# Two key chunks of x loaded one by one, and six steps' attention numerators formed by features in column tiles

## The chip, the cores and the metric

The kernel runs on one core of a Trainium2 chip. The metric is the time of one execution in device microseconds; the time before is the median of three runs. The core has a matrix engine (TensorE; PE in the profile, its weight loads PEld), a vector engine (VectorE, DVE), an engine for activations (ScalarE, ACT), GpSimd (POOL) and a queue engine that issues transfers (SyncE, SP). TensorE multiplies a stationary operand (the weights, loaded first) by a moving one, column by column, and writes to PSUM, a memory of eight banks of 512 float32 per partition.

## The reference

Two attention blocks read the same x (2048 tokens, 640 features, 32 heads of 20 features), and a gate mixes their outputs.

```python
g = sigmoid((x * gate_w).sum(-1))                 # one gate per token
# block A: linear attention, features softmax(p) and softmax(-p), p = (q or k) @ w_phi
kv, z = sum_s phi_k[s] v[s], sum_s phi_k[s]
a = (phi_q @ kv / (phi_q @ z + 1e-6)) @ wo_A
# block B: four segments of 512 tokens
logits = q @ k.T * 20**-0.5 + causal_mask         # within the segment
a_dot = softmax(logits) @ v
a_mem = (phi(q) @ M) / (phi(q) @ z + 1e-6)        # phi(t) = t + 1 if t > 0 else exp(t)
o = sig(beta) * a_mem + (1 - sig(beta)) * a_dot   # then M, z += phi(k).T v, sum phi(k)
b = o @ wo_B
out = g * a + (1 - g) * b
```

## The kernel before, in words

Every engine executes its instructions in the order in which the program emits them (`manual_schedule`), so the order of the work is written out by hand. The parts, in order of time:

**The start (to about 11 us).** The key weights come in five chunks of 128 rows (`wnat_k`, three on ScalarE's queue, two on SP's), and the first 512 tokens of x are wanted as keys early. A string of two-letter steps (line 319) lists the work of the start: `T` transposes a weight chunk on TensorE (line 181) and copies it out, `M` multiplies a transposed chunk with the masked `w_phi` (line 189; "the fold"), `X0` transposes two key chunks of x (line 200), `k` and `v` are the key and value products of a chunk (line 242). The letter `a` or `d` behind a number says whether ScalarE or VectorE copies the result out. x for `X0` comes in one load on SP's queue (line 107), behind `w_phi` and two weight chunks and ahead of the gate vector, the value weights (line 111) and the transposing loads of x (line 114). All PSUM tiles of this part come from one pool, `aps`, of four pairs of banks, and a tile takes a pair that came free.

**Block A (to about 127 us).** For 16 chunks, keys and values, their exponentials (line 253) and normalised features (line 261); then the sums `kv` (line 393, where TensorE is split into two column tiles of 64 columns), query features (line 420), and numerators and denominators (lines 478, 496). For the last of these the pool `aps` is closed and four others take its banks, `nps0`, `nps1` and `nps2` for numerators and `pps` for projections of block B; they lie in the order in which a tuple lists them.

**Block B (127 to 303 us).** There are 32 steps: four segments by eight groups of four heads. Two steps make a double step, 16 of them. A double step emits five bursts of scores: each burst is two PSUM tiles filled by products with 32 rows (line 757, four row tiles) and read by one exponential each on ScalarE (line 761, 128x1024); GpSimd then clears the triangle above the diagonal (line 768). The probabilities of a step are kept by key chunk, keys on the partitions: chunk c against the queries from 128c on.

Between the bursts stand items from a string per double step (`PLAN`, line 971): `A` to `D` are the numerators and memory products of a step, `h` halves of the next segment's projections (line 943), `f` and `o` halves of the output projections (line 887), `t` a transposing transfer of finished output rows, `x`, `y`, `k`, `q` and `z` parts of the feature maps. `A` and `D` belong to the first step of the double step, `B` and `C` to the second step of the double step before. Each item has a weight in microseconds, and `SHARES` says what share of the weights may be emitted before each next burst.

The numerators of a step (`pv_items`, line 811) are, for four query chunks j and four heads i, products over the key chunks c up to j: 40 in all, with 128 probabilities as weights and 21 columns moving (20 value features and a column of ones, whose sum is the denominator). Results have queries on the partitions, in one bank of the tile `nda`. The other bank takes the memory products (`mem_items`, lines 819 and 824). Then `emit_epi` divides: a reciprocal (line 836), a product with the gates (838), the scaling of both parts (848, on VectorE) and their sum into `oB` (851, mostly GpSimd); for three segments it also updates the memory (854 to 858).

**The end (303 us on).** `u` in the plan issues four transposing transfers (line 981) of the last segment's first 384 output columns, which the last products (line 1067) read; the last step and the last rows follow.

Of the kernel before, what the change touches and what calls it, by code (L numbers as in the profile page):

```python
# [15 lines left out]
def kernel(  # L16
# [82 lines left out]
    nc.sync.dma_start(out=Wc, in_=A_w_phi.rearrange("h f g -> (h f) g").rearrange("(c p) g -> p c g", p=P))  # L99

    for what in "w1 w3 x0 g v0 v1".split():
        n = int(what[1:]) if len(what) > 1 else 0
        if what[0] == "w":
            nc.sync.dma_start(out=wnat_k[:, n], in_=wsrc(D)[:, n])
        elif what[0] == "x":
            x_nat[n] = xload.tile([P, 2, D], BF16, name="x_nat")
            nc.sync.dma_start(out=x_nat[n], in_=x2[0:512].rearrange("(m r) d -> m r d", r=4)[:, 2 * n:2 * n + 2])
# [44 lines left out]
    for j, eng in ((0, nc.vector), (1, nc.gpsimd), (2, nc.vector), (3, nc.gpsimd), (4, nc.gpsimd)):  # L152
        emit_Wphi(j, eng)
# [21 lines left out]
    def w2tile(name):  # L175
        return aps.tile([P, 2, 512], F32, name=name, tag="w2")
# [18 lines left out]
    def emit_xT(n):  # L195
        pair = w2tile("xtp")
        tps = [pair[:, u].bitcast(BF16)[:, 0:D].rearrange("p (c t) -> p c t", c=KC) for u in range(2)]
        for u in range(2):
            for c in range(KC):
                nc.tensor.transpose(out=tps[u][:, c, :], in_=x_nat[n][:, u, c * P:(c + 1) * P], identity=ident_b)  # L200
        for u in range(2):
            nc.vector.tensor_copy(out=xP[:, :, (2 * n + u) * P:(2 * n + u + 1) * P], in_=tps[u])
# [116 lines left out]
    for step in "T0a T2d M0a T1d M2a T4d M1a T3d X0 M4a M3a k0 g k1 v0 v1 r0 r1".split():  # L319
        n = int(step[1:2] or 0)  # L320
        if step[0] == "T":
            emit_foldT(wnat_k, WkT, n, {"a": nc.scalar.copy, "d": nc.vector.tensor_copy}[step[2]])
        elif step[0] == "M":
            emit_foldM(WkT, WkA, n, {"a": nc.scalar.copy, "d": nc.vector.tensor_copy}[step[2]])
        elif step[0] == "X":
            emit_xT(n)
        elif step[0] == "k":
# [130 lines left out]
    vBs = [resB.tile([P, 4, H, DH + 1], BF16, name=f"vB{n}") for n in range(2)]  # L458
# [110 lines left out]
    def emit_zsum():  # L569
        emit_zz(emit_z(z_den[:, 0]))  # L570
        open_stages()
        for vB in vBs:
            nc.gpsimd.memset(vB[:, :, :, DH:DH + 1], 1.0)

# [5 lines left out]
    for what in "ppppvzppppdvp":  # L580
# [16 lines left out]
        for n in ('nps1', 'pps', 'nps0', 'nps2')}  # L597
# [109 lines left out]
    with ExitStack() as bctx:  # L707
# [7 lines left out]
            for n in ('bnd', 'st_b', 'bps', 'st_a')}  # L715
# [18 lines left out]

        class Step:
            def __init__(self, k):
                self.s, self.g = divmod(k, G)
                self.PT = {}
                self.last = k == NSEG * G - 1
                self.nda = nda  # L740
# [73 lines left out]

        def mem_items(st):
# [15 lines left out]
        def emit_epi(st):  # L831
# [14 lines left out]
            else:  # L846
# [4 lines left out]
                eng.tensor_tensor(out=oview, in0=tdv[:, 0], in1=tdv[:, 1], op=ALU.add)  # L851
            if s < NSEG - 1:
# [84 lines left out]

        def half_item(part, sc, half):
# [17 lines left out]
        def half_items(s, order):  # L956
# [14 lines left out]
        PLAN = ("qhhhyzhokxooAD", "qhhByhChkzoxAooD", "qhhByhChkzxoAooD",  # L971
                "ooBqoyokCozxoADo", "hkhBhhChhqhyAhDztt", "khhBxhhqChfhyzAD",
                "khhBxhhqCfyzADt", "khhBxhhqChfyhzAD", "khhxtBhhqChyhADzt",
                "hhBhhqChfyhzAD", "hhBhhqCfhyzAthD", "hhBhhqhCftyhzAD",
                "fBftCfftAD", "ffBtCfftAD", "fBtfCffADf", "fBCuffAffD")
        SHARES = [[0.2, 0.42, 0.55, 0.78], [0.19, 0.4, 0.6, 0.84], [0.2, 0.4, 0.6, 0.81], [0.19, 0.38, 0.59, 0.78], [0.19, 0.38, 0.58, 0.81], [0.18, 0.41, 0.65, 0.86], [0.2, 0.4, 0.6, 0.83], [0.19, 0.4, 0.6, 0.83], [0.2, 0.4, 0.6, 0.8], [0.22, 0.39, 0.6, 0.82], [0.19, 0.39, 0.61, 0.82], [0.2, 0.39, 0.6, 0.82], [0.2, 0.4, 0.6, 0.8], [0.21, 0.4, 0.61, 0.8], [0.19, 0.37, 0.59, 0.82], [0.2, 0.41, 0.6, 0.84]]
# [10 lines left out]
        for dstep in range(NSEG * G // 2):  # L987
# [5 lines left out]
            for w in PLAN[dstep]:  # L993
# [177 lines left out]
```

## Time and profile before

| | |
|---|---|
| median of 3 runs | 316.44 us (316.29 to 316.65) |
| profiled execution | 315.58 us |
| its span in the profile | 313.6 us |
| TensorE, ScalarE busy | 303.6 us, 252.0 us |
| VectorE, GpSimd busy | 224.0 us, 206.8 us |
| granted TensorE clock | 1.0 |

A row of a group shows the line, engine and operation, the tile written and those read, shapes, then the count, busy time and the mean duration in ns of one; behind the second bar stands the idle time of the engine just before, and what ended it. A row of the timeline starts with the start and the length in us from the span's start; a number after `x` says how many instructions were merged. Matmuls overlap and their ends are modelled, so the price of a run of them is read from its first start to the start of what follows.

### The profile page before, as it was taken

What the parts mean: (1) busy time and instruction counts of PE and PEld (TensorE: products, weight loads), DVE (VectorE), ACT (ScalarE), POOL (GpSimd) and SP (SyncE); (2) the same over time, 40 slices, a digit from 0 to 9 for tenths busy, and PEclk for the clock granted to TensorE, in tenths of its full rate; (3) what the DMA queues carried; (4) which work ended last, traced back from release to release, by engine and by line L of the source; (5) the groups of instructions that cost most, each with busy time, mean ns of one, the idle gap of its engine ahead of it and who ended that gap; (6) DMA issues with size and microseconds to landing.
All of it is one profiled execution on the core that took longest, in us unless ns stands there. A gap on an engine that the chain in (4) does not pass through costs nothing.

```text
span 313.6 us, 10096 instructions
## 1 busy us (share of the span) xinstructions
PE 303.6 (97%) x4182; PEld 208.4 (66%) x4182; DVE 224.0 (71%) x508; ACT 252.0 (80%) x320; POOL 206.8 (66%) x308
## 2 busy tenths in 40 slices
PE   8999999999999999999999999999999999999995
PEld 7788877755578778465666666565666666565673
DVE  3477997999779997677758588777755765455553
ACT  4677888267846648999998999999998898998953
POOL 8588599103247989955657577688786877666550
PEclk9999999999999999999999999999999999999999
DMA  7989944439217998775421394473745545222132
GB/s 216 199 184 204 210 108 129 127 89 365 74 36 106 130 136 147 135 100 99 55 50 36 69 127 86 59 120 69 110 84 78 86 100 72 64 78 53 48 90 84
DMA packets 94007, 34.56 MB, mean 110 GB/s; under 512 B 82442, under 2 KB 93834, under 8 KB 93962
## 3 DMA queue, kind: packets, MB, share of 16 engines
q1 hardware_dynamic: 93386, 33.28, 54.4%
q10 hardware_dynamic: 576, 0.66, 0.7%
q8 instruction: 32, 0.52, 0.7%
q14 instruction: 13, 0.11, 0.1%
HBM read 6.10 MB, written 2.62 MB: 28 GB/s over the span
## 4 chain that ended last, share of the span: by engine, by line
PE 69%; ACT 19%; DVE 4%; POOL 3%; issue 2%; DMA 1%; ACTq 0%; DVEq 0%; POOLq 0%
ACT PT L761 16%; PE proj L943 10%; PE st_ps L757 10%; PE proj L887 9%; PE pk L242 7%; PE pq L420 7%; PE nda L811 7%; PE pv L242 7%; PE proj L557 3%; PE num L478 2%; PE kv_ps L393 2%; DVE tt L527 1%; DMA oTA<-oA 1%; POOL oA L686 1%; DVE rr L503 1%
## 5 line engine op out<-in xcount | busy, mean ns | idle before, releaser
L761 ACT ACTIVATE PT<-st_ps 128x1024 bf16<-128x1024 f32 x160 | 153.9, 1023 | 12.2 <-PE st_ps L757 9.8
L768 POOL TENSOR_SCALAR_AFFINE_SELECT PT<-PT 128x512 bf16<-128x512 bf16 (+1 forms) x130 | 84.4, 668 | 46.7 <-ACT PT L761 46.3
L811 PEld LDWEIGHTS <-PT 128*128 128x128 bf16 x1280 | 40.0, 96 | 9.0 <-issue 5.4
L811 PE MATMUL nda<-vB,PT 128*128 128x21 bf16 x1240 | 41.5, 173 | 0.1
L261 POOL TENSOR_TENSOR EkSn<-Ek,krec 128x1280 bf16<-128x1280 bf16 x15 | 35.1, 2360 | 9.2 <-DVE krec L260 7.3
L943 PEld LDWEIGHTS <-xTf 128*128 128x128 bf16 x300 | 26.5, 97 | 13.8 <-issue 5.3
L949 DVE CAST Z<-proj 128x320 bf16<-128x320 f32 x44 | 21.1, 488 | 16.7 <-PE proj L943 15.6
L427 ACT ACTIVATE Eq<-pq 128x1024 bf16<-128x1024 f32 x20 | 19.4, 1021 | 12.2 <-PE pq L420 12.2
L257 DVE TENSOR_REDUCE ksum<-Ek 128x64 f32<-128x1280 bf16 x16 | 23.6, 1474 | 7.2 <-ACT Ek L253 7.2
L527 DVE TENSOR_TENSOR tt<-num,rr 128x640 f32<-128x640 f32 x32 | 25.0, 812 | 4.6 <-POOL rr L520 1.8
L686 POOL TENSOR_TENSOR oA<-tt 128x640 bf16<-128x640 f32 x16 | 24.6, 1545 | 5.3 <-DVE tt L527 5.0
L887 PE MATMUL proj<-WkA,oTA 128*128 128x320 bf16 x160 | 28.0, 300 | 0.0
L757 PE MATMUL st_ps<-Z 32*128 32x512 bf16 (+3 forms) x256 | 24.9, 299 | 3.0 <-ACT PT L761 2.5
L253 ACT ACTIVATE Ek<-pk 128x640 bf16<-128x640 f32 x32 | 20.8, 703 | 7.9 <-PE pk L242 6.8
L757 PE MATMUL st_ps<-Eq 32*128 32x512 bf16 (+3 forms) x256 | 25.2, 299 | 1.5 <-ACT PT L761 1.2
L242 PEld LDWEIGHTS <-xTf 128*128 128x128 bf16 x200 | 22.6, 113 | 4.7
L851 POOL TENSOR_TENSOR oB<-td 128x320 bf16<-128x320 f32 x22 | 19.6, 889 | 4.4 <-DVE td L848 3.6
L420 PE MATMUL pq<-xTf,WqA 128*128 128x512 bf16 x100 | 22.4, 379 | 0.0
L887 PE MATMUL proj<-WvA,oT 128*128 128x320 bf16 x120 | 21.3, 300 | 0.0
L848 DVE TENSOR_TENSOR td<-nda,rec 128x640 f32<-128x640 f32 x23 | 19.0, 825 | 2.5 <-DVE rec L838 0.5
L836 DVE RECIPROCAL rec<-nda 128x32 f32<-128x32 f32 (+1 forms) x31 | 10.3, 331 | 12.8 <-PE nda L824 8.1
L887 PEld LDWEIGHTS <-oTA 128*128 128x128 bf16 x160 | 13.6, 97 | 8.3 <-issue 4.2
(183 smaller groups left out, 558.8 us busy)
## 6 DMA issues: line engine op xcount, KB each, us to landing
Z<-EkSn SPq DMA_DIRECT2D x32, 160.0 KB, 2.8
out_dram<-orow SPq DMA_DIRECT2D x8, 160.0 KB, 1.9
out_dram<-oTA SPq DMA_DIRECT2D x6, 160.0 KB, 1.8
WvA<-in_A_wqkv_dram SPq DMA_DIRECT2D x2, 400.0 KB, 6.4
WvB<-in_B_wv_dram SPq DMA_DIRECT2D x1, 800.0 KB, 4.7
WkB<-in_B_wk_dram SPq DMA_DIRECT2D x1, 800.0 KB, 6.5
WqB<-in_B_wq_dram SPq DMA_DIRECT2D x1, 800.0 KB, 8.2
WkA<-in_A_wo_dram SPq DMA_DIRECT2D x1, 800.0 KB, 11.3
```

What stands on the lines that cost most here:

```text
L242: nc.tensor.matmul(ps[:, bk, 0:n], lhsT=key_tokens(c, sc), rhs=rhs, start=(c == 0), stop=(c == by_row[-1][0] if sc == 0 and W is WkA else ...
L257: nc.vector.tensor_reduce(out=ksum, in_=Ek.rearrange("p s (h f) -> p (s h) f", f=DH), axis=AX.X, op=ALU.add)
L261: (nc.vector if sc == NCH - 1 else nc.gpsimd).tensor_tensor(out=EkSn[:, sc].rearrange("p s (h f) -> p (s h) f", f=DH), in0=Ek.rearrange("p ...
L420: nc.tensor.matmul(pq[:, half, :], lhsT=WqA[:, c, j * P:(j + 1) * P], rhs=xq[:, 2 * qb + half, c], start=(c == 0), stop=(c == KC - 1))
L527: nc.vector.tensor_tensor(out=tt[:, sgn].rearrange("p (b h) d -> p b h d", b=2), in0=ps, in1=csb, op=ALU.mult)
L686: nc.gpsimd.tensor_tensor(out=oA.rearrange("p (h d) -> p h d", d=DH), in0=tt[:, 0], in1=tt[:, 1], op=ALU.add)
L757: nc.tensor.matmul(ps[:, i - i0, o:o + L - c * P], lhsT=kT[32 * i:32 * i + 32, c * P:(c + 1) * P], rhs=qT[32 * i:32 * i + 32, c * P:L], st ...
L761: nc.scalar.activation(out=PT[:, i0:i0 + 2], in_=ps, func=ACT.Exp, scale=SCALE_B)
L768: nc.gpsimd.affine_select(out=v, in_=v, pattern=[[0, n_i], [1, P]], compare_op=ALU.is_ge, fill=0.0, base=0, channel_multiplier=-1)
L811: nc.tensor.matmul(nd[:, j, i], lhsT=block(st, c)[:, i, (j - c) * P:(j - c + 1) * P], rhs=vB[:, c, 4 * st.g + i, :], start=(c == 0), stop= ...
L887: nc.tensor.matmul(ps, lhsT=oT[:, k % KC], rhs=W[:, k % KC, hs], start=(k == 0), stop=(k == n - 1))
L943: nc.tensor.matmul(ps, lhsT=xq[:, sc // 4, k, sc % 4 * P:(sc % 4 + 1) * P], rhs=W[:, k, half * 320:(half + 1) * 320], start=(k == 0), stop ...
```

## The change

The start: the two key chunks get a load and a tile each, issued one after the other at the place of the one load; each is transposed (five products) and copied out by itself, and `X1` stands behind the fold of chunk 4. The transposes of weight chunk 3 (`T3d`) go ahead of the fold of chunk 1 (`M1a`). VectorE's two masked pieces of `w_phi` become a step `P` at the head of the list, and the load of `w_phi` a step `c`.

Block B: for six steps (`TURNED`) the numerators are formed by features. For each key chunk and head, 32 columns of the value tile (21 of the head's own, the rest of the next head's or of a cleared strip behind the last) are the weights, in column tile i of TensorE, and the probabilities of the chunk move past them, up to 512 queries at a time: 16 products. The result has features on the partitions, four heads of 32 rows, and fills one bank. VectorE casts it to bf16, a transposing transfer on SP's queue turns it so that queries are on the partitions, and the scaling of this part and the sum into `oB` are put off: `run_fins` does them at the end of the next turned step, or ahead of the next other step. The memory part is scaled at once. Such a step's memory products go before its numerators, and all of it stands at `A` or `B`; its `C` or `D` is empty. The value tiles get 12 more columns, cleared by GpSimd. The four PSUM pools of block A's end and those of block B are listed in another order, and the strings of the plan and the shares are changed.

```diff
-    for what in "w1 w3 x0 g v0 v1".split():
+    for what in "c w1 w3 x0 x1 g v0 v1".split():
...
-            x_nat[n] = xload.tile([P, 2, D], BF16, name="x_nat")
-            nc.sync.dma_start(out=x_nat[n], in_=x2[0:512].rearrange("(m r) d -> m r d", r=4)[:, 2 * n:2 * n + 2])
+            x_nat[n] = xload.tile([P, D], BF16, name="x_nat")
+            nc.sync.dma_start(out=x_nat[n], in_=x2[0:512].rearrange("(m r) d -> m r d", r=4)[:, n])
...
     def emit_xT(n):
...
+        tp = w2tile("xtp")[:, 0].bitcast(BF16)[:, 0:D].rearrange("p (c t) -> p c t", c=KC)
+        for c in range(KC):
+            nc.tensor.transpose(out=tp[:, c, :], in_=x_nat[n][:, c * P:(c + 1) * P], identity=ident_b)
+        nc.vector.tensor_copy(out=xP[:, :, n * P:(n + 1) * P], in_=tp)
...
-    for step in "T0a T2d M0a T1d M2a T4d M1a T3d X0 M4a M3a k0 g k1 v0 v1 r0 r1".split():
+    for step in "P T0a T2d M0a T1d M2a T4d T3d M1a X0 M4a X1 M3a k0 g k1 v0 v1 r0 r1".split():
...
-        for n in ('nps1', 'pps', 'nps0', 'nps2')}
+        for n in ('nps0', 'nps2', 'pps', 'nps1')}
...
-            for n in ('bnd', 'st_b', 'bps', 'st_a')}
+            for n in ('bps', 'st_a', 'st_b', 'bnd')}
...
+        TURNED = {22, 24, 25, 26, 27, 28}
+        fins_due = []
...
+        def turned_items(st):
+            def mm():
+                for c in (0, 1, 3, 2):
+                    for i in range(4):
+                        o = (c * H + 4 * st.g + i) * (DH + 1)
+                        nc.tensor.matmul(st.nda[32 * i:32 * i + 32, 0, c * P:L], lhsT=vBf[st.s % 2][:, o:o + 32],
+                                         rhs=block(st, c)[:, i, 0:L - c * P], start=(c == 0), stop=(c == 2),
+                                         tile_position=(0, 32 * i))
+                LTs.append(LTs.pop(0))
+                LT = LTs[-1] if LTs[-1] is not None else bw.tile([P, L], BF16, name="LT", bufs=1)
+                nc.vector.tensor_copy(out=LT, in_=st.nda[:, 0])
+                st.LN = bw.tile([P, 4, P], BF16, name="LN", bufs=2)
+                nc.sync.dma_start_transpose(out=st.LN, in_=LT)
+                emit_epi_turned(st)
+                run_fins(1)
+            return mem_items(st)[:-1] + [(0.73, mm)]
+
+        def emit_epi_turned(st):
...
+            def scale(n, den, v, eng):
+                recv = rec[:, n].rearrange("p (j i) -> p j i", j=4)
+                nc.vector.reciprocal(out=recv, in_=den)
+                nc.vector.tensor_tensor(out=recv, in0=recv, in1=og[:, n, :, 4 * g:4 * g + 4], op=ALU.mult)
+                eng.tensor_tensor(out=td[:, n].rearrange("p (j i) d -> p j i d", j=4), in0=v,
+                                  in1=recv[:, :, :, None].to_broadcast([P, 4, 4, DH]), op=ALU.mult)
...
+            scale(1, mv[:, :, :, DH], mv[:, :, :, 0:DH], nc.vector)
+
+            def fin():
+                lv = st.LN.rearrange("p j (i e) -> p j i e", i=4)
+                scale(0, lv[:, :, :, DH], lv[:, :, :, 0:DH], nc.vector)
+                tdv = td.rearrange("p n (j i) d -> p n j i d", j=4)
+                nc.gpsimd.tensor_tensor(out=oBs[s][:, :, g * 80:(g + 1) * 80].rearrange("p j (i d) -> p j i d", d=DH),
+                                        in0=tdv[:, 0], in1=tdv[:, 1], op=ALU.add)
+            fins_due.append(fin)
+            emit_state(st)
...
-                "hhBhhqChfhyzAD", "hhBhhqCfhyzAthD", "hhBhhqhCftyhzAD",
-                "fBftCfftAD", "ffBtCfftAD", "fBtfCffADf", "fBCuffAffD")
+                "hhBhhqChfhyzAD", "hhBhhqCfhyhzAtD", "hhBhhqhCfthyzAD",
+                "ffBtCfftAD", "ffBtCffADt", "fBtCfffADf", "fBCufffAfD")
...
-                    items += pv_items(st, (0, 1, 2)) if w in "AB" else pv_items(st, (3,)) + mem_items(st)
+                    if st.turned:
+                        items += turned_items(st) if w in "AB" else []
+                    else:
+                        items += ([(0.0, run_fins)] + pv_items(st, (0, 1, 2)) if w in "AB"
+                                  else pv_items(st, (3,)) + mem_items(st))
```

More of the change, by code (lines that the diff above doesn't have):

```diff
@@ L150, in emit_Wphi @@
                                 op=ALU.mult)
-    for j, eng in ((0, nc.vector), (1, nc.gpsimd), (2, nc.vector), (3, nc.gpsimd), (4, nc.gpsimd)):
-        emit_Wphi(j, eng)
+    for j in (1, 3, 4):
+        emit_Wphi(j, nc.gpsimd)
     for sgn in range(2):
@@ L326 @@
             emit_xT(n)
+        elif step[0] == "P":
+            for j in (0, 2):
+                emit_Wphi(j, nc.vector)
         elif step[0] == "k":
@@ L457 @@
     resB = ctx.enter_context(tc.tile_pool(name="resB", bufs=1))
-    vBs = [resB.tile([P, 4, H, DH + 1], BF16, name=f"vB{n}") for n in range(2)]
+    VW = 4 * H * (DH + 1)
+    vBf = [resB.tile([P, VW + 12], BF16, name=f"vB{n}") for n in range(2)]
+    vBs = [t[:, 0:VW].rearrange("p (c h e) -> p c h e", c=4, h=H) for t in vBf]
     a3e = a3_stack.enter_context(tc.tile_pool(name="a3e", bufs=KC, side="right", reuse_waits="tile"))
@@ L571, in emit_zsum @@
         open_stages()
-        for vB in vBs:
+        for vB, vf in zip(vBs, vBf):
             nc.gpsimd.memset(vB[:, :, :, DH:DH + 1], 1.0)
+            nc.gpsimd.memset(vf[:, VW:VW + 12], 0.0)
     def emit_first_den():
@@ L739, in __init__ @@
                 self.last = k == NSEG * G - 1
+                self.turned = k in TURNED
                 self.nda = nda
@@ L936, in run_first, with run_fins @@
                 fns.pop(0)()
+        def run_fins(keep=0):
+            while len(fins_due) > keep:
+                fins_due.pop(0)()
         def half_item(part, sc, half):
```

29 lines of the change are left out of this document (16 added, 13 removed).

## The prediction

> **What bounds the kernel now.** I read the page first: the busy times, then the slices, for the stages in which TensorE and ScalarE are full.
>
> ```profile
> PE 303.6 (97%) x4182; PEld 208.4 (66%) x4182; DVE 224.0 (71%) x508; ACT 252.0 (80%) x320; POOL 206.8 (66%) x308
> ...
> PE   8999999999999999999999999999999999999995
> ...
> ACT  4677888267846648999998999999998898998953
> PEclk9999999999999999999999999999999999999999
> ```
>
> TensorE is full nearly everywhere, at full clock. From slice 17 on (127 us, the attention part) ScalarE is full too, so the question there is which of the two is late. Next I asked for busy time by stretches, one for each of the double steps 11 to 15 (a double step is two steps, ten exponentials on ScalarE; I cut at the start of its first), and for what ScalarE's exponentials wait for in them.
>
> ```profile
> core 0: us, PE busy (x) PEld busy (x) DVE busy (x) ACT busy (x) POOL busy (x), PEclk, DMA share, GB/s
> 248.13:259.40 11.27, 11.27 (x170) 7.39 (x168) 7.88 (x17) 10.24 (x11) 8.11 (x15) 1.00 0.78 109
> 259.40:270.80 11.40, 11.37 (x167) 7.19 (x166) 5.36 (x12) 9.69 (x11) 8.51 (x17) 1.00 0.27 62
> 270.80:281.16 10.36, 10.15 (x152) 6.08 (x150) 5.10 (x10) 9.69 (x11) 6.30 (x11) 1.00 0.26 65
> 281.16:292.00 10.84, 10.55 (x155) 6.38 (x154) 5.78 (x12) 9.66 (x11) 6.52 (x10) 1.00 0.28 73
> 292.00:303.00 11.00, 10.80 (x160) 7.12 (x160) 5.19 (x13) 9.62 (x11) 7.32 (x13) 1.00 0.27 67
> ...
> ACT PT L761 <- PE st_ps L757: 5.3, 15, 0.5
> ```
>
> In 11 and 12 TensorE has no idle time at all; in 13 to 15 it has 0.2 to 0.3 us. ScalarE has 1.03, 1.71, 0.67, 1.18 and 1.38 us to spare (11.27 less 10.24, and so on), and the last row (248 to 303 us) puts 5.3 us of its waits on scores that TensorE brings late. So here time taken off TensorE shortens the kernel, up to ScalarE's spare time; VectorE is half idle.
>
> **The numerators of six steps.** Today a step's numerators are 40 products with the probabilities as weights and 21 columns moving. Steps 22, 24, 25, 26, 27 and 28 get 16 products instead (a double step works on the numerators of its own first step and of the second step before it, so 22 falls in double step 11, 24 in 12, 25 and 26 in 13, 27 and 28 in 14): 32 columns of values as weights in one of four column tiles, 512, 384, 256 or 128 queries moving.
>
> ```profile
> 265.05 0.84 PE L887 MATMUL proj<-WkA,oTA 128*128 128x320 bf16 x5
> 265.82 0.45 PE L757 MATMUL st_ps<-Eq 32*128 32x512 bf16 x4
> 266.20 0.85 PE L887 MATMUL proj<-WvA,oT 128*128 128x320 bf16 x5
> 266.89 0.84 PE L887 MATMUL proj<-WkA,oTA 128*128 128x320 bf16 x5
> ...
> 279.41 1.16 PE L811 MATMUL nda<-vB,PT 128*128 128x21 bf16 x40
> 280.42 0.31 PE L819 MATMUL nda<-Mbd,xTf 128*128 128x84 bf16 x4
> ```
>
> ```profile
> 57.15 3.85 PE kv_ps L393 x181
> ...
> 65.02 8.65 PE pq L420 x40
> ```
>
> The price today is 280.42 less 279.41, 1.01 us, 25 ns a product. For the new form no row exists, so I build it. A column moving takes 8.65 us / 40 / 512 = 0.422 ns. One column tile sees 512+384+256+128 = 1280 columns, 0.54 us, if the four tiles run side by side; 5120 columns, 2.16 us, if they do not. Do they? Four row tiles do: 4 x 512 columns would take 0.86 us in a row, and 265.82 to 266.20 is 0.38 us. Two column tiles do: the kv products (row L393 in the chain, tiles of 64 columns, nearly all with 80 columns moving) take 3.85/181 = 21.3 ns with their weight load, where 80 columns alone take 33.8. That leaves four column tiles likely and unproven. A change of tiling costs too: five products before the scores take 265.82 less 265.05 = 0.77 us against 266.89 less 266.20 = 0.69, so 0.08 to go in, and 0.38 less 0.216 = 0.16 for the scores above their own columns. With 0.24 us for both, a turned step costs 0.78 us and saves 0.23. Ends: 0.54 us (a change of tiling that the neighbouring scores pay anyway), saving 0.47, and 2.16 + 0.24 = 2.40 us, losing 1.39. I take 0.78, because the row that it is nearest to is the four-tile one. The Trainium skill, "TensorE: Matmul & The Clock Gate", Part 3, states 3.07 times for four row tiles at 512 columns and 2.38 times for three column tiles; my estimate by the 3.07 of that page is 0.70 us, a saving of 0.31 a step, and no run here shows it yet.
>
> What of it is on the path: 0.23 us in double steps 11 and 12 each (step 23 keeps the old form), where TensorE is full, so 0.46; 0.46 in 13, where ScalarE's spare 0.67 includes handovers that stay (its waits are 5.3/15 = 0.35 us each), so I take 0.3; 0.46 in 14, spare 1.18, so I take 0.45. Sum 1.2 us.
>
> **What the turned form adds elsewhere.** VectorE and DMA rows, by shape:
>
> ```profile
> L898 DVE CAST orow<-proj 128x320 bf16<-128x320 f32 x16 | 7.9, 491 | 14.9 <-PE proj L887 14.6
> L848 DVE TENSOR_TENSOR td<-nda,rec 128x640 f32<-128x640 f32 x23 | 19.0, 825 | 2.5 <-DVE rec L838 0.5
> L844 DVE TENSOR_TENSOR oB<-nda,rec 128x320 bf16<-128x320 f32 x8 | 3.9, 492 | 0.3
> L836 DVE RECIPROCAL rec<-nda 128x32 f32<-128x32 f32 x23 | 8.2, 357 | 9.7 <-PE nda L824 5.3 <-PE nda L819 4.3
> L836 DVE RECIPROCAL rec<-nda 128x16 f32<-128x16 f32 x8 | 2.0, 256 | 3.1 <-PE nda L824 2.8
> L838 DVE TENSOR_TENSOR rec<-rec,Eq 128x32 f32<-128x32 f32 x23 | 7.3, 316 | 1.0
> L838 DVE TENSOR_TENSOR rec<-rec,Eq 128x16 f32<-128x16 f32 x8 | 1.7, 208 | 0.3
> ...
> oT<-oB SPq DMA_TRANSPOSE x12, 2.7
> ...
> 294.23 5.08 SPq L981 DMA_TRANSPOSE oTA<-oB  x4
> 302.11 0.78 PEld L1067 LDWEIGHTS <-oTA 128*128 128x128 bf16 x6
> ```
>
> VectorE today: 0.36 + 0.32 + 0.83 = 1.50 us a step. New: a cast of 512 columns (estimate 0.69, from 0.49 at 320 and 0.83 at 640), then 0.26 + 0.21 + 0.49 for the memory part and the same 0.96 for the local part, 2.6 us: 1.1 more, 2.2 in double step 13, on 5.10 of 10.36. It is hidden by VectorE's idle half. Should that cover go, projection buffers come free late: there are two, so a projection needs the cast of the one two before it. In double step 14 a long one (10 products, 1.38 us) and two short ones (0.69) follow a turned step; the second short one needs a cast that ends 2.6 + 0.49 = 3.1 us after the turned products, and TensorE gets to it after 1.38 + 0.69 and a burst of scores (0.38 and 0.24), 2.7: at most 0.4 us of stall. GpSimd's addition stays (same shape, later). The new transposes are six on SP's queue; landing 2.7 us, about 3.4 us or more before the local part is scaled, since that is put off to the next turned step. The tightest is step 28: its local part now ends beside step 29, and the four transposes of the last segment (issued 294.23, 5.08 us long, first read at 302.11) wait for it. Between the end of their issue, 299.31, and 302.11 lie 2.8 us, of which the last one's landing takes about 1.4 (2.7 from its issue, less 5.08/4); a microsecond later costs nothing. The bank for numerators comes free after the cast (0.69 us) and no longer after the scaling (1.50). The two cleared strips of 12 columns run on GpSimd at a time when it waits: nothing.
>
> **The start.** One load of two key chunks becomes two, ten transposes become five and five, and the transposes of weight chunk 3 go ahead of the fold of chunk 1.
>
> ```profile
> 2.35 0.43 SPq L107 DMA_DIRECT2D x_nat<-in_A_x_dram  x1
> ...
> 7.58 0.32 PEld L181 LDWEIGHTS <-wnat_k 128*128 128x128 bf16 x5
> 7.88 0.57 PEld L200 LDWEIGHTS <-x_nat 128*128 128x128 bf16 x10
> 8.41 0.84 PEld L189 LDWEIGHTS <-WkT 128*128 128x128 bf16 x20
> ...
> 9.05 1.29 ACT L193 CAST WkA<-fold_ps 128x640 bf16<-128x640 f32 x2 [0.53 <-PE fold_ps L189]
> ```
>
> ```profile
> 4.27 13.75 SPq L114 DMA_TRANSPOSE xTf<-in_A_x_dram  x3
> ...
> DMA to landing us min/median/max: 10.2/10.2/10.2
> ...
> 14.84 11.18 PEld L242 LDWEIGHTS <-xTf 128*128 128x128 bf16 x82
> ```
>
> From 7.58 us on TensorE runs without a gap to speak of, and nothing is taken off it, so the order alone gains only where an eviction is late: the last fold's leaves ScalarE at 10.34 and the last key products of chunk 0 need it then. The new order brings the last two evictions about 0.25 us forward, of which 0.1 us reaches the key products. Against it, the second load issues 0.43 us more on SP's queue, ahead of gate vector, value weights and the transposes of x. The first of those, issued at 4.27, lands at 14.47 and is first read at 14.84; a shift of 0.43 eats the 0.37 of slack. The two cancel: 0, between -0.3 and +0.3. The two masks now emitted in the step list keep their place on VectorE's queue, as nothing of VectorE stood between.
>
> **Buffers and plan.** The order of the PSUM pools changes.
>
> ```profile
> 88.33 0.93 PE L478 MATMUL num<-kvn,Eq 128*128 128x140 bf16 x20
> 88.53 1.94 ACT L427 ACTIVATE Eq<-pq 128x1024 bf16<-128x1024 f32 x2 [1.46 <-PE pq L420]
> 90.52 0.54 PE L478 MATMUL num<-kvn,Eq 128*128 128x140 bf16 x10
> ```
>
> Only the pair of banks that ScalarE reads until 90.47 can hold anything up. Today the pool nps2, first used at 90.52, lies there. The extra transposed tile moves every later tile to another pair, and followed by the order in which the four come free the late pair falls on nps2 again; the pools of the last part keep their pairs relative to these. So 0; if I followed it wrongly, the first numerators wait from 88.33 to 90.47, +2.1 us at most. The small moves in the plan of double steps 0 to 10 shift an item by one burst each; there I take 0, within 0.3 us either way.
>
> **Sum.** 1.2 us off. The profiled execution took 315.58 us (span 313.6, 1.98 around it); it would take 314.4, its span 312.4. It lies 0.86 under the median of 316.44, which becomes 315.2.
>
> **Rivals.** (1) The turned steps save time on TensorE and ScalarE takes it up: its idle time before exponentials is the handover itself. Speaks for it: in double step 13 it has only 0.67 us spare. Against: 12 and 14 have 1.71 and 1.18. It gives 0.4 us, 316.0, no measurable change (a difference under 0.2%, 0.63 us, is about what a measurement here can't tell from none). (2) The other side: the four column tiles run only two at a time. Then the products take 1.08 + 0.24 = 1.32 us, 0.31 more than today, on a full TensorE: 6 x 0.31 = 1.9 us, 318.3. It decides at 2.16/(1.01 - 0.24) = 2.8 tiles at once: above that a gain, below a loss. For it: L393 shows two at once and reaches 33.8/21.3 = 1.6 of 2, but at 21 ns a pair is near the 25 of the numerators' pairs, so likely held by issue. Against: the scores' four row tiles. (3) The 16 weight loads are not hidden behind the streams. At the 21.3 ns that load and product take together in L393, 16 of them add at most 0.34 us: 1.12 us a step, 0.11 more than today, 0.7 us in six, 317.1. Against: in L393 the loads do hide, as 21.3 ns is below the 33.8 of the stream alone. The Trainium skill, "TensorEngine Tiling (Array Packing)", Gotcha 2, says column tiling and Fast Weight Load exclude one another; that is what would slow these loads, and L393's 21.3 ns, measured with column tiles, speaks against its mattering.
>
> **How the numbers follow.** The forecast (faster by 0.7 to 2.3 us) has 0.72; rival 1 0.13; rival 2 0.09; rival 3 and a mistaken buffer together 0.06. Faster is 0.72, the same 0.13, slower 0.15. The likeliest case's own range is 314.1 to 315.8: 0.54 us per turned step and ScalarE's spare time as its limit give 2.3 off; 0.6 is its other end. The range asked for takes in the start's and the plan's 0.3 each at the low end, and rival 1 and what lies up to half a microsecond above today's time at the high end: 313.6 to 316.9. Left out are rival 2, rival 3 and the far tail of the low side, together under 0.2.
>
> **What would show it.** Right: 16 products on a line of the new function within 0.7 to 0.8 us before the next group; double steps 11 to 14 at about 11.0, 11.2, 10.1 and 10.4 us, 15 unchanged; ScalarE's waits for scores in 248 to 303 us down from 5.3 to some 4.2; the key products of chunk 0 ending within 0.3 us of 10.8; first numerators right behind the last query products. Wrong: the sixteen products taking over 1.0 us; a wait of VectorE for the new transpose, with casts and projections behind it; a wait at 88 us or at 14.8 us.

## The result, and the profile after

The changed kernel took 313.94 us (median of 15 runs, 313.23 to 314.52), the kernel before, on the same chip, 315.43 (15 runs, 314.28 to 316.76): a ratio of 0.9943, 95% interval 0.9928 to 0.9958. Two later comparisons gave 0.9946 (0.9926 to 0.9966) and 0.9957 (0.9944 to 0.9970). So the change takes about 0.5% off; by the medians of the three comparisons it is 1.5 to 1.7 us. The two profiled executions took 315.58 and 314.52 us, with spans of 313.6 and 312.8; they show 0.8 to 1.1 us of it. Where the rest lies stays open: the stretch before the first attention exponential varies from 126.3 to 127.6 us over the 14 profiles of this document, without an order by kernel, and single executions can't settle half a microsecond there.

The page of the changed kernel has these busy times and slices:

```profile
PE 302.4 (97%) x4038; PEld 205.3 (66%) x4038; DVE 230.3 (74%) x532; ACT 251.9 (81%) x320; POOL 205.6 (66%) x310
...
PE   8999999999999999999999999999999999999995
...
ACT  4677888357956549899999899999998999899953
PEclk9999999999999999999999999999999999999999
```

144 matmuls are gone (six times 40 less 16), TensorE is busy 1.2 us less and VectorE 6.3 us more, 1.05 a turned step. Next the stretches of double steps 11 to 15, and what waited between 248 and 303 us (total, times, longest):

```profile
core 0: us, PE busy (x) PEld busy (x) DVE busy (x) ACT busy (x) POOL busy (x), PEclk, DMA share, GB/s
248.38:259.54 11.16, 11.08 (x146) 6.78 (x144) 6.97 (x16) 10.29 (x12) 7.69 (x14) 1.00 0.70 104
259.54:270.63 11.09, 11.09 (x142) 6.60 (x140) 7.20 (x18) 9.69 (x10) 8.83 (x18) 1.00 0.46 75
270.63:280.72 10.09, 9.44 (x104) 4.78 (x102) 6.00 (x16) 9.53 (x10) 5.48 (x10) 1.00 0.40 93
280.72:291.13 10.41, 10.11 (x107) 5.10 (x106) 7.44 (x21) 9.68 (x11) 6.52 (x11) 1.00 0.43 104
291.13:302.30 11.17, 11.04 (x160) 7.31 (x160) 7.75 (x19) 9.70 (x11) 8.14 (x14) 1.00 0.25 50
```

```profile
ACT PT L774 <- PE st_ps L770: 4.4, 14, 0.5
...
DVE rec L855 <- DMA LN<-LT: 1.4, 1, 1.4
...
DVE rec L855 <- DMA LN<-zt: 1.0, 1, 1.0
```

Double steps 11 to 14 went from 11.27, 11.40, 10.36 and 10.84 us to 11.16, 11.09, 10.09 and 10.41: 1.12 us less (1.07 by the starts of the exponentials to the hundredth). In 13 TensorE now idles 0.65 us where it idled 0.21, and ScalarE has 0.56 us to spare: that double step is nearly at ScalarE's limit. Double step 15 did not keep its length: from the start of its first exponential to the start of its last it took 10.07 us instead of 9.92. New are the two waits of VectorE for turned numerators; the later one matters, as shown below.

The sixteen products, in the timeline of TensorE of the changed kernel:

```profile
279.57 0.73 PE L833 MATMUL nda<-PT,vB 128*32 128x512 bf16 x16
280.23 0.74 PE L770 MATMUL st_ps<-Eq 32*128 32x512 bf16 x4
```

From their first start to that of the scores behind them is 0.66 us, where 40 products took 1.01; the other five turned steps show 0.66 to 0.67. Between these two points all six save 2.1 us of TensorE's time; what the groups beside them pay is counted further down.

### The profile page after: what moved, and what is told of

Its sections match the earlier page's. It is cut to its first block, busy times and chain, and to the rows that moved or that the text cites. A ratio compares the mean times of both kernels' runs of the same rounds, so it can differ in the third digit from the quotient of the medians.

```text
span 312.8 us, 9844 instructions
## 1 busy us (share of the span) xinstructions
PE 302.4 (97%) x4038; PEld 205.3 (66%) x4038; DVE 230.3 (74%) x532; ACT 251.9 (81%) x320; POOL 205.6 (66%) x310
## 4 chain that ended last, share of the span: by engine, by line
PE 68%; ACT 21%; DVE 5%; POOL 3%; issue 2%; ACTq 0%; DVEq 0%; POOLq 0%
ACT PT L774 18%; PE proj L1008 10%; PE st_ps L770 9%; PE proj L948 8%; PE pq L421 7%; PE pk L240 7%; PE pv L240 7%; PE nda L824 5%; PE proj L561 3%; DVE tt L531 2%; PE num L482 2%; PE kv_ps L394 2%; DVE rr L507 2%; POOL oA L691 1%; PE warm L316 1%
## 5 line engine op out<-in xcount | busy, mean ns | idle before, releaser
L824 PEld LDWEIGHTS <-PT 128*128 128x128 bf16 x1040 | 32.9, 96 | 7.8 <-issue 4.5
L1008 PEld LDWEIGHTS <-xTf 128*128 128x128 bf16 x300 | 26.5, 97 | 14.1 <-issue 5.5
L824 PE MATMUL nda<-vB,PT 128*128 128x21 bf16 x1000 | 34.2, 173 | 0.0
L770 PE MATMUL st_ps<-Eq 32*128 32x384 bf16 (+3 forms) x256 | 25.6, 298 | 1.9 <-ACT PT L774 1.5
L240 PEld LDWEIGHTS <-xTf 128*128 128x128 bf16 x200 | 22.6, 113 | 4.7
L561 PEld LDWEIGHTS <-xTf 128*128 128x128 bf16 x180 | 15.8, 97 | 4.6
L770 PEld LDWEIGHTS <-Z 32*128 32x128 bf16 x256 | 7.5, 91 | 16.2 <-issue 15.0
L482 PEld LDWEIGHTS <-Eq 128*128 128x128 bf16 x320 | 15.9, 96 | 3.3 <-issue 0.7
```

The source lines that it names most:

```text
L240: nc.tensor.matmul(ps[:, bk, 0:n], lhsT=key_tokens(c, sc), rhs=rhs, start=(c == 0), stop=(c == by_row[-1][0] if sc == 0 and W is WkA else ...
L561: nc.tensor.matmul(ps, lhsT=xq[:, sc // 4, cc, sc % 4 * P:(sc % 4 + 1) * P], rhs=W[:, cc, half * 320:(half + 1) * 320], start=(cc == 0), s ...
L770: nc.tensor.matmul(ps[:, i - i0, o:o + L - c * P], lhsT=kT[32 * i:32 * i + 32, c * P:(c + 1) * P], rhs=qT[32 * i:32 * i + 32, c * P:L], st ...
L824: nc.tensor.matmul(nd[:, j, i], lhsT=block(st, c)[:, i, (j - c) * P:(j - c + 1) * P], rhs=vB[:, c, 4 * st.g + i, :], start=(c == 0), stop= ...
L1008: nc.tensor.matmul(ps, lhsT=xq[:, sc // 4, k, sc % 4 * P:(sc % 4 + 1) * P], rhs=W[:, k, half * 320:(half + 1) * 320], start=(k == 0), stop ...
```

## The experiments

Two lengths are used below, both from the starts of exponentials in ScalarE's timeline. "Last part" is from the first exponential of double step 11 to the start of the last one of double step 15: 53.74 us before, 52.82 in the changed kernel. "Attention" is the same from double step 0 on: 174.99 and 173.99.

**Only the start and the pools.** No step is turned, and the plan and shares are those of before.

```diff
-        TURNED = {22, 24, 25, 26, 27, 28}
+        TURNED = set()
# PLAN and SHARES: those of the kernel before
```

> The changed kernel with no turned step and the plan and shares of before: what is left is the start (two loads, the order of transposes and folds), the pools' order and the longer value tiles. If the column tiles carry the gain: within 0.2% of before (ratio 0.998 to 1.002), the first exponential of keys within 0.1 us of 10.86, the first score exponential within 0.5 us of 126.88. If the start carries a good part: ratio 0.997 or below.

Measured: 314.94 us against 315.28, ratio 0.9993 (0.9976 to 1.001); the last part 53.73 us. The first attention exponential starts at 127.44 us, 0.56 after that of the kernel before and just outside what was put down, but within the spread of 126.3 to 127.6. The start, taken alone, brings nothing that can be told.

**Start, pools and the new plan, no step turned.**

```diff
-        TURNED = {22, 24, 25, 26, 27, 28}
+        TURNED = set()
```

> The changed kernel with no turned step, but with its own plan and shares. If the column tiles carry the gain: ratio to before 0.998 to 1.002 again, double steps 11 to 14 as before (11.3, 11.4, 10.4, 10.8 us). If the new plan carries a good part by itself: ratio 0.997 or below, and those double steps shorter by 0.2 us or more.

Measured: 315.71 us, ratio 1.0009 (0.9989 to 1.003), the last part 53.77 us. Double steps 11 to 14 did not stay as they were: they took 11.37, 11.14, 10.69 and 10.64 us, against 11.28, 11.39, 10.36 and 10.80 before (all by the starts of the exponentials). The plan moves up to 0.3 us from one to another; their sum stays (43.84 and 43.83 us), so the moves bring nothing by themselves. What the last part lost is the work of the turned steps.

**Everything but the start.** Loads, order and transposes of x as before, and with them the old order of the pools, which fits the old number of tiles.

```diff
-    for what in "c w1 w3 x0 x1 g v0 v1".split():
+    for what in "w1 w3 x0 g v0 v1".split():
...
-    for step in "P T0a T2d M0a T1d M2a T4d T3d M1a X0 M4a X1 M3a k0 g k1 v0 v1 r0 r1".split():
+    for step in "P T0a T2d M0a T1d M2a T4d M1a T3d X0 M4a M3a k0 g k1 v0 v1 r0 r1".split():
...
-        for n in ('nps0', 'nps2', 'pps', 'nps1')}
+        for n in ('nps1', 'pps', 'nps0', 'nps2')}
```

> The changed kernel with the loads, the order of the start and the pools' order of before; turned steps, plan and shares stay. If the column tiles carry the gain: ratio to before 0.993 to 0.997, as the whole change has (0.9943). If start and turned steps share it: 0.997 to 1.000.

Measured: 314.48 us, ratio 0.9979 (0.9964 to 0.9994); the last part 52.94 us, so the turned steps' gain is all there. The ratio alone would leave 0.3% to the start, which the start alone had not shown. That was tried again at the end.

**Sixteen products head by head.** The same products, but all four of a column tile one after the other, so that the program's order no longer goes round the tiles.

```diff
-                for c in (0, 1, 3, 2):
-                    for i in range(4):
+                for i in range(4):
+                    for c in (0, 1, 3, 2):
```

> The same 16 products a turned step, in another order: all four of one head, so of one column tile, then the next head's. If column tiles run side by side only when neighbouring products go to different ones: 5120 columns in a row, 2.16 us and a change of tiling in place of 0.66 us, so 1.5 to 1.7 us more a step, 9 to 10 us in six on TensorE, of which some 7 to 9 reach the end: ratio to before 1.015 to 1.025. If the order does not matter (the 0.66 us has another reason than side by side): ratio as the whole change, 0.994.

A miss. Measured: 314.28 us, ratio 0.9976 (0.9958 to 0.9994), the last part 52.95 us. The timeline of TensorE of this kernel:

```profile
279.16 0.76 PE L833 MATMUL nda<-PT,vB 128*32 128x512 bf16 x16
279.85 0.68 PE L770 MATMUL st_ps<-Eq 32*128 32x512 bf16 x4
```

The scores that follow start 0.69 us behind the first product, against 0.66. In the records the first products of the four heads start 13 ns apart, though four lie between them in the program; in the changed kernel the four start 3.3 ns apart. So each column tile takes up its own products whatever the order in which they come, here at least over 16 of them, and the order is worth 0.03 us a step.

**The changed kernel again,** beside the next three.

> The changed kernel itself, beside the others on the same chip. By the traces so far, double steps 11 to 15 give 0.9 us and the double steps before them and the end 0.1 each, the start nothing: ratio to before 0.996 to 0.997. If the whole 0.9943 of its first runs is real: 0.993 to 0.995.

Measured: 314.1 us against 315.76, ratio 0.9946 (0.9926 to 0.9966), the second of the two values put down; the last part 53.23 us, its double steps 11 to 14 as in the first profile to 0.02 us, and double step 15 10.47 us.

**The old order of the pools alone.**

```diff
-        for n in ('nps0', 'nps2', 'pps', 'nps1')}
+        for n in ('nps1', 'pps', 'nps0', 'nps2')}
...
-            for n in ('bps', 'st_a', 'st_b', 'bnd')}
+            for n in ('bnd', 'st_b', 'bps', 'st_a')}
```

> The changed kernel with the order of the PSUM pools of before. If the extra transposed tile moves the late pair of banks and the new order follows it, as I had it: the first numerators or projections wait for ScalarE's last query exponentials, up to 2.1 us from 88.5 us on, of which 0.5 to 2 reach the end: 0.002 to 0.006 above the changed kernel. If the order makes no difference: equal to it.

Measured: 315.24 us, ratio 0.9991 (0.9973 to 1.001), 0.0045 above the changed kernel. The timeline of this kernel:

```profile
87.95 1.94 ACT L428 ACTIVATE Eq<-pq 128x1024 bf16<-128x1024 f32 x2 [1.41 <-PE pq L421]
...
89.94 1.52 PE L561 MATMUL proj<-WkB,xTf 128*128 128x320 bf16 x10 [1.26 <-ACT Eq L428]
```

With the old order the late pair of banks falls to the projections' pool: TensorE waits 1.26 us for the last exponentials of the query features (which end at 89.89), and block B starts that much later (38.6 us from the start of the last of those exponentials to the first attention exponential, against 37.3). Everything after it has its usual length. So the new order of the pools is no gain of its own: it undoes a loss that the new start would bring.

**Eight turned steps, and twelve.** Steps 18 and 20 besides, one in a double step; then 16 to 21, two in a double step.

```diff
-        TURNED = {22, 24, 25, 26, 27, 28}
+        TURNED = {18, 20, 22, 24, 25, 26, 27, 28}
```

> Steps 18 and 20 are turned as well (first steps of double steps 9 and 10, where TensorE is full and VectorE 7.8 of 11.4 us busy). If TensorE's time is what counts there and VectorE's idle time covers 1.1 us more: 0.25 to 0.35 us off each, double steps 9 and 10 shorter by that, 0.5 to 0.7 us below the changed kernel. If VectorE's cover is gone: equal to it or above.

```diff
-        TURNED = {22, 24, 25, 26, 27, 28}
+        TURNED = {16, 17, 18, 19, 20, 21, 22, 24, 25, 26, 27, 28}
```

> Steps 16 to 21 are turned as well: two in each of double steps 9 and 10, one in 8 and one in 11. VectorE then has 10 of 11 us to do. If it still covers: 1.5 to 2 us below the changed kernel. If its cover is gone: projections wait for their casts, and it is equal to the changed kernel or up to 2 us above, with waits of TensorE on VectorE in 200 to 250 us.

Measured: 313.85 us, ratio 0.9932 (0.9911 to 0.9953), for eight; 318.12 us, ratio 1.0079 (1.0052 to 1.0106), for twelve. Eight stand 0.25 us below the changed kernel, within the noise and short of the 0.5 to 0.7 put down; twelve stand 4.0 above it, outside the 2 put down. Attention took 174.01 us with eight, as long as with six: double step 9 became 0.08 us shorter, 10 became 0.22 longer, 11 0.06 longer and 15 0.16 shorter. In 10 VectorE waits 1.21 us for the transposed numerators of step 18, which are wanted ahead of step 19's, and TensorE waits 0.21 for a memory update. With twelve attention took 179.73. Some 1.5 us of that belong to double step 7, where the granted clock was 0.84 for a stretch (203 to 214 us) in this execution, and not to the edit; double steps 9 to 11, at full clock, grew by 1.99, 1.24 and 1.05 us against the changed kernel. The stretch 225 to 236 us, in the changed kernel first, then the kernel with twelve:

```profile
225.00:236.00 11.00, 10.97 (x167) 7.10 (x164) 6.51 (x17) 9.84 (x12) 8.73 (x17) 1.00 0.55 104
```

```profile
225.00:236.00 11.00, 8.46 (x103) 4.64 (x102) 8.97 (x21) 7.88 (x10) 8.37 (x15) 1.00 0.49 89
```

TensorE falls from full to 8.46 us, VectorE rises to 8.97. Who keeps TensorE waiting is in the timeline of the kernel with twelve, VectorE and TensorE:

```profile
226.87 0.67 DVE L838 CAST LT<-nda 128x512 bf16<-128x512 f32 x1
...
228.73 0.23 DVE L915 TENSOR_TENSOR mtmp<-nda,CM 128x84 f32<-128x84 f32 x1
...
233.21 0.62 DVE L857 TENSOR_TENSOR td<-LN,rec 128x320 f32<-128x320 bf16 x1
233.75 0.87 DVE L1014 CAST Z<-proj 128x320 bf16<-128x320 f32 x2
```

```profile
229.02 0.31 PE L876 MATMUL nda<-Mbd,xTf 128*128 128x84 bf16 x4 [1.02 <-DVE mtmp L915]
...
234.28 0.84 PE L1008 MATMUL proj<-WvB,xTf 128*128 128x320 bf16 x5 [1.05 <-DVE Z L1014]
```

From 226.87 to 234.6 VectorE works with one pause of 0.77 us. A product that updates the memory (`mtmp`, needed by the next step's memory products) and two casts of projections (whose buffers the next projections need) stand behind the chains of the turned steps, and each costs TensorE a microsecond. That is the price of the cover: where a double step already has casts of projections, one turned step about evens out (0.08 us gained in one, 0.22 lost in another), and two cost one to two microseconds.

**Once more, on one chip: the changed kernel, the old start, the start alone, eight turned steps.** The edits are those above.

> The changed kernel again, beside the start taken back and the start alone, all on one chip. Two readings of the earlier ratios are to be told apart. First: the new start is worth nothing, and the ratio of 0.998 for the kernel with the old start came from the chip or the hour. Then this kernel and the one with the old start stand within 0.0015 of each other, at some 0.995 to 0.997. Second: the new start is worth 0.3% together with the turned steps. Then this kernel stands at 0.994 to 0.995 and the one with the old start 0.003 above it.

> The changed kernel with the old loads, the old order of the start and the old order of the pools. If the start is worth nothing: within 0.0015 of the changed kernel run beside it. If it is worth 0.3%: 0.003 above it, and in the profile x arrives late for its transposes (0.2 us or more) or the first key products end 0.25 us or more later after the first transposes of weights.

> The new start alone, without turned steps and with the old plan. If the start is worth nothing: 0.9985 to 1.0015 of the kernel before. If it is worth 0.3%: 0.996 to 0.998.

> Eight turned steps instead of six (18 and 20 besides). From the profile of its first run, in which the stretch from the first attention step to the last exponential was as long as in the changed kernel (174.0 us in both), I expect it within 0.001 of the changed kernel run beside it. If the two further steps bring what the six brought a step (0.15 us each), it is 0.001 below.

Measured against 315.36 us: 313.80 (ratio 0.9957, 0.9944 to 0.9970), 314.29 (0.9968, 0.9952 to 0.9985), 315.04 (0.9992, 0.9979 to 1.0006) and 313.75 (0.9956, 0.9941 to 0.9972). The old start stands 0.0011 above the new one, within what was put down for "worth nothing"; the earlier gap of 0.003 did not come back. So the start can't be told from nothing here, and no profile shows a place for a gain. Eight turned steps are as good as six.

**Double step 15, across these profiles.** No run was made for it; seven profiles of kernels with exactly these six turned steps and two with eight lie side by side. Without turned steps it takes 9.92 or 9.93 us, with the new plan too. With six it takes 10.07 to 10.47, and VectorE waits 1.0 to 1.4 us for the transposed numerators of step 28 in every one. With eight it takes 9.91, and VectorE does not wait; with twelve it is the same. All these lengths go from the start of its first exponential to the start of its last. VectorE, SP's queue and GpSimd in the changed kernel (`LT` and `zt` are the two buffers that the cast of the numerators uses in turn):

```profile
293.17 0.47 DVE L959 CAST orow<-proj 128x320 bf16<-128x320 f32 x1
294.69 0.26 DVE L855 RECIPROCAL rec<-LN 128x16 f32<-128x16 bf16 x1 [1.04 <-DMA LN<-zt]
```

```profile
290.69 1.19 SPq L840 DMA_TRANSPOSE LN<-zt  x1
```

```profile
295.76 0.87 POOL L867 TENSOR_TENSOR oB<-td 128x320 bf16<-128x320 f32 x1 [1.38 <-DVE td L857]
296.58 1.22 POOL L781 TENSOR_SCALAR_AFFINE_SELECT PT<-PT 128x512 bf16<-128x512 bf16 x2
```

VectorE gets to the put-off part 3.0 us after the transpose was issued and waits until 4.0 us after it. GpSimd's sum waits for VectorE, and the clearing of two triangles, without which those probabilities can't be used, stands behind the sum on its queue. TensorE feels it in a group of numerators, here in the changed kernel and then in that with eight turned steps:

```profile
298.77 0.92 PE L824 MATMUL nda<-vB,PT 128*128 128x21 bf16 x24
```

```profile
298.09 0.76 PE L824 MATMUL nda<-vB,PT 128*128 128x21 bf16 x24
```

In the records of the first the fifteenth product starts 0.17 us after the one ahead of it, at 299.27, just behind the end of a clearing at 299.22, while the others stand 0.025 apart; in the second that clearing was over before the group began, and the gap is not there. These 0.15 us are what the double step grew by. In the second profile of the changed kernel the wait is 1.44 us, and TensorE is reached through VectorE too, by the additions that free projection banks (VectorE, then TensorE):

```profile
295.88 0.25 DVE L855 RECIPROCAL rec<-LN 128x16 f32<-128x16 bf16 x1 [1.44 <-DMA LN<-zt]
...
298.72 0.48 DVE L957 TENSOR_TENSOR oTA<-proj,oTA 128x320 bf16<-128x320 f32 x1
```

```profile
299.25 0.84 PE L948 MATMUL proj<-WvA,oT 128*128 128x320 bf16 x5 [0.20 <-DVE oTA L957]
```

With eight turned steps the same transpose landed in 2.4 us instead of 4.0 (issue, count, us to landing; first the changed kernel, then that with eight), and the put-off part started without a wait:

```profile
LN<-zt SPq DMA_TRANSPOSE x1, 4.0
```

```profile
LN<-zt SPq DMA_TRANSPOSE x1, 2.4
```

```profile
292.49 0.47 DVE L959 CAST orow<-proj 128x320 bf16<-128x320 f32 x1
292.89 0.23 DVE L855 RECIPROCAL rec<-LN 128x16 f32<-128x16 bf16 x1
```

That the wait lengthens double step 15 is read from nine profiles that agree, not from a run that removes it alone.

## Why the prediction was right, point by point

Forecast was a time 0.39% shorter, for the turned steps and nothing else; measured were 0.43 to 0.57% in three comparisons. The time of 315.2 lies above what was measured mostly because the kernel before took 315.4 in these runs and not 316.44. The cause is as forecast: the turned steps shorten the last part by 0.5 to 0.9 us in all seven profiles, the other parts of the change by nothing that a run could tell.

**The price of a turned step** was right for a step by itself. The 0.66 us from the first product to the start of what follows hold 0.55 us of streams (in the records the last of the four groups of products starts 0.44 us after the first, and its 256 columns take 0.11 at 0.422 ns a column) and 0.11 to leave the column tiles. What it costs to go into them falls on the group ahead:

```profile
279.32 0.32 PE L876 MATMUL nda<-Mbd,xTf 128*128 128x84 bf16 x4
279.57 0.73 PE L833 MATMUL nda<-PT,vB 128*32 128x512 bf16 x16
...
294.41 0.31 PE L876 MATMUL nda<-Mbd,xTf 128*128 128x84 bf16 x4
294.56 0.57 PE L948 MATMUL proj<-WvA,oT 128*128 128x320 bf16 x3
```

Four memory products take 0.25 us ahead of the sixteen and 0.15 ahead of projections, so 0.10 to go in. The whole is 0.76, where 0.78 was taken. One of the six steps stands between memory products and projections and saves the 0.25 us that this leaves. The other five stand beside scores, which change the tiling themselves (memory products right ahead of scores take 0.24 us too, in the kernel with the new plan and no turned step), and save 0.35 each, through what the prediction's better end called "a change of tiling that the neighbouring scores pay anyway". That makes 2.0 us in six, 1.9 by the table below, where 1.4 were forecast. 5120 columns, 2.16 us one after the other, take 0.66 from first start to next start: 3.3 times. The Trainium skill, "TensorE: Matmul & The Clock Gate", Part 3, states 3.07 for four row tiles, by which the estimate was 0.70; the 0.66 of four column tiles is a little better than that.

**What of it reached the path** was judged too favourably. Predicted off double steps 11 to 14: 0.23, 0.23, 0.3 and 0.45, in sum 1.2 us out of 1.4 saved on TensorE. Measured by the starts of the exponentials: 0.12, 0.29, 0.27 and 0.39, in sum 1.07 out of 1.9. That the sums are so close is luck: more was saved than forecast, and less of it arrived. Nor do the single double steps speak for the forecast, because the new plan alone had already moved them; against the kernel with that plan and no turned step the four became 0.21, 0.04, 0.60 and 0.23 us shorter. Where the rest went is in the records, if each product is given the time from its start to the start of the next one. From the first exponential of double step 11 to that of 15 this gives (us; groups cut at the two ends make the sums differ by up to 0.06):

| | before | new plan, no turned step | changed |
|---|---|---|---|
| numerators | 8.40 | 8.40 | 6.17 |
| memory products and updates | 2.01 | 2.01 | 2.32 |
| projections | 21.47 | 21.24 | 21.15 |
| scores | 11.90 | 12.25 | 13.07 |
| the whole stretch | 43.82 | 43.84 | 42.75 |

The numerators lost 2.2 us. 0.3 came back as the change into the column tiles, and 0.8 to 1.2 in the scores. Scores need a PSUM tile that an earlier exponential has read, and the page's busy time hides much of that wait:

```profile
271.91 0.39 PE L770 MATMUL st_ps<-Eq 32*128 32x128 bf16 x4
272.62 0.39 PE L770 MATMUL st_ps<-Eq 32*128 32x128 bf16 x4 [0.32 <-ACT PT L774]
```

The second group's first product starts 0.65 us after the last of the first group, and only 0.32 us of that count as idle. It starts 0.05 us behind the end of an exponential. In the changed kernel 18 products within bursts start 0.050 to 0.052 us behind an exponential's end, and the gaps ahead of them sum to 5.3 us; before there were 18 with 4.1 us, with the plan alone 15 with 4.7. So the prediction's reading that TensorE "has no idle time at all" in double steps 11 and 12 took waiting for work (0.9 and 0.8 us of the 4.1 lie there), and 0.6 to 1.2 us of what was saved became more of this waiting: for that part rival 1 holds, that ScalarE takes the saving up. ScalarE's own waits for scores fell from 5.3 to 4.4 us (4.2 expected).

One sum of the prediction does not come out: with 0.47 us saved a step and ScalarE's spare time as the limit, double steps 11 to 14 give 0.47, 0.47, 0.67 and 0.94, which is 2.5 us and not 2.3.

**Double step 15 unchanged** was wrong: 0.15 us longer, up to 0.55 in other profiles of the same kernel. The step that failed is the transposes' slack, "about 3.4 us or more before the local part is scaled": for step 28 VectorE was there after 3.0 us, and the landing took 4.0 to 4.4, not 2.7. The prediction had named step 28 as the tightest, but looked for the damage at the tail's four transposes. Those were indeed issued 2.4 us later (296.65, not 294.23), and the tail did not grow (11.60 us from the start of the last exponential to the end, 11.73 before). The damage came through the queues of VectorE and GpSimd, the place that the prediction listed under "wrong".

**VectorE's work** was right: 1.05 us more a step by the busy time, 1.1 predicted, and the cast took 0.69, as estimated. No projection waited in double step 14. That the idle half of VectorE is the cover, and that projections are what fails without it, the kernel with twelve showed: four microseconds lost in three double steps, at the buffers named.

```profile
L857 DVE TENSOR_TENSOR td<-LN,rec 128x320 f32<-128x320 bf16 x6 | 3.3, 544 | 0.2
...
L838 DVE CAST zt<-nda 128x512 bf16<-128x512 f32 x3 | 2.1, 692 | 1.5 <-PE nda L833 1.5
```

**Start, pools and plan at nothing** held. The first exponential of keys starts at 10.90 us (10.86 before), the transposes of x are issued at 4.72 (4.27; 0.43 later predicted) and nothing waits for them; first numerators and projections follow the query products without a gap. That the order of the pools had been followed rightly is shown by its undoing: 1.26 us of wait, within the 2.1 put down as the most.

**Rivals 2 and 3.** Four column tiles work side by side: 2.16 us of columns pass in 0.55 us of streams, 3.9 at once, well above the 2.8 at which the gain would vanish. Nor do the weight loads show (weight loads of the sixteen products: count, shortest, median and longest in ns, then first and last start):

```profile
L833 PEld LDWEIGHTS <-vB x96: 92/97/98, 258.4 to 289.6; 128*32 128x32 bf16 x96
```

They last as long as those of 128 columns (97 ns on the page's groups) and lie beside the streams; before all 96 together the engine sat idle 0.2 us. The Trainium skill, "TensorEngine Tiling (Array Packing)", Gotcha 2, has column tiling exclude Fast Weight Load; if that slows these loads, 0.66 us a step shows no cost of it.

## What to carry to other kernels

Price a new form from rows of the same engine in another tiling, and then ask how much of the saving the next engine will swallow: here the form cost what was priced, its neighbours made it cheaper, and some two fifths of the saving never reached the end. A full row of busy time does not show that an engine never waits; compare the starts of its instructions with the ends of those that they need. When a result is put off behind a transfer, compare its slack with the longest landing seen and list what stands behind the waiting instruction on that engine and on the engines that it feeds. And count the cover by stretch: beside VectorE's casts of projections one turned step per double step brought between 0.08 us gained and 0.22 lost, two cost one to two microseconds.

## What had not been expected of the hardware

The column tiles run independently over at least sixteen products: with the program's order head by head they start 13 ns apart and the group takes 0.69 us, with the order round the tiles 3.3 ns and 0.66. Going from one tiling to another shows as 0.09 to 0.10 us more between the last product of a group and the first of the next (memory products: 0.13 us ahead of turned products or scores, 0.04 ahead of projections).

A transposing transfer of one size (128x512) from SP's queue lands in 2.4 us most times (2.4, 2.4, 2.4 and 2.5 of six in the changed kernel) and in 3.3 and 4.0 for two. In the six profiles with the same plan and steps that follow the first, VectorE again waits for the transfer of step 28, 1.1 to 1.4 us; with eight turned steps it is others that land in 3.3 to 4.5. The packets are not what is slow. In the changed kernel the stretches around it (last three columns: clock, busy share of the DMA engines, GB/s) are

```profile
292.00:293.00 1.00, 1.00 (x10) 0.72 (x8) 0.97 (x3) 1.00 (x2) 0.57 (x2) 1.00 0.63 130
293.00:294.00 1.00, 1.00 (x33) 0.77 (x31) 0.65 (x2) 0.54 (x2) 1.00 (x2) 1.00 0.00 0
294.00:295.00 1.00, 1.00 (x30) 0.76 (x26) 0.28 (x2) 1.00 (x2) 0.38 (x1) 1.00 0.00 0
```

so the last packet had moved by 293.0, and VectorE went on at 294.69. What held it back in between stays open: by the profile's reading it is this transfer, and which transfer is late changed with the number issued before it.
